# Startup of a fused attention and gMLP block: modulation weight rows, a turned conditioning vector, and separate banks for the first query copies

## Chip, cores, metric

One core of one Trainium2 chip. The metric is device time in microseconds of one execution. Times of one kernel spread by 0.7 us between its first three runs.

In the lines of the profile PE is TensorE, PEld its weight loads, DVE VectorE, ACT ScalarE, POOL GpSimd and SPq the queue of SyncE, which issues most transfers. L763 is line 763 of that run's kernel; the line numbers shift a little from kernel to kernel. A bank is a tile of 128 x 512 f32 in PSUM, where every matmul of this kernel writes its result. An x tile is 128 rows of x, and to turn a tile is to transpose it.

## The reference, cut to what matters

```python
mod = (_silu(c) @ w_mod).reshape(c.shape[0], 6, 1, -1)      # c: 1 x 512, w_mod: 512 x 3072
sa, ca, ga, sb, cb, gb = ...                                # six rows of 512
h = _layernorm(x) * (1 + ca) + sa                           # x: 1 x 2048 x 512
x = x + ga * _A_ref(h, K, V, wq, wo)                        # 32 query heads, 8 key heads, Dh 128
h = _layernorm(x) * (1 + cb) + sb
x = x + gb * _B_ref(h, w_in, w_sp, b_sp, w_out)             # gMLP
```

Nothing of the attention can start before the first two rows of `mod` (shift and scale) are known, the first 128 rows of x are normalised, modulated and turned, and their queries are projected. That preparation is what the change touches.

## The kernel before

The DMA loads of the start, in issue order. The modulation weight is read so that partition p holds rows 4p to 4p+3; c is read to match, eight bytes per partition:

```python
wmod_dram = w_mod.rearrange("(p dt) n -> p dt n", p=P)
c_dram = c[0].rearrange("(p j) -> p j", p=P)
...
nc.scalar.dma_start(out=c_bf[:], in_=c_dram)
nc.sync.dma_start(out=x_sb[:, 0, :], in_=x_dram[:, 0, :])
for kt in range(NDT):                                   # four parts of 256 KB
    nc.sync.dma_start(out=wmod_a[:, kt, :], in_=wmod_dram[:, kt, 0 : 2 * D])
load_k_nat(0)
...
load_wq(0, nc.sync)                                     # first query weights, 512 KB
load_k_nat(1)
nc.sync.dma_start(out=x_sb[:, 1:CT, :], in_=x_dram[:, 1:CT, :])
```

The in-order matmul program of the start. `warm(n)` issues n matmuls on zeros, whose result nobody reads; they are meant to keep TensorE's clock up. `bank("misc")`, `bank("o_ps")` and `bank2()` each rotate through two buffers, so what is written to a buffer waits until the readers of its last contents are done:

```python
warm(10)
for kt in range(NDT - 1):
    mod_part(kt, mc_ps)                                 # 8 matmuls of one column
    warm(2)
x_ps = []                                               # turn the normalised x tile 0
for half in range(2):
    x_ps.append(bank(("misc", "o_ps")[half])[:].bitcast(BF16))
    ...                                                 # two transposes each
mod_part(NDT - 1, mc_ps)
mod_copy(0, mc_ps)                                      # VectorE: shift and scale
...                                                     # hT: VectorE two blocks, ScalarE two
k_turn((0, 1, 2, 3), (nc.vector.tensor_copy, nc.scalar.copy))   # first keys
q_ps = bank2()                                          # ONE tile of two banks
for n, dt in enumerate((0, 2, 1, 3)):
    for hh in range(REP):
        c0 = hh // 2 * 512 + hh % 2 * P
        nc.tensor.matmul(q_ps[:, c0 : c0 + P], ...)     # 16 matmuls: first queries
for hf, copy in enumerate((nc.vector.tensor_copy, nc.scalar.copy)):
    copy(out=qTs[0][:, 2 * hf : 2 * hf + 2, 0:P], in_=q_ps[:, hf * 512 : ...])
warm(1)
```

After that the attention loop runs: scores, exponential, values, with the preparation of x tiles 1 to 3 filled in between.

## Time and profile before

| | before |
|---|---|
| time, median (lowest to highest) | 1325.91 us (1325.71 to 1326.42), 3 runs |
| span of the profiled run | 1324.6 us |
| TensorE busy | 99% |
| ScalarE, VectorE, GpSimd busy | 81%, 36%, 4% |
| TensorE's share of the chain that ended last | 98% |

The chain that ended last is followed back from the last instruction: at each step to whatever released it. Where TensorE carries 98% of it, the program is one stream of matmuls, and a change elsewhere can count only if it makes the stream start earlier or run with fewer gaps. The lines themselves stand in the prediction.

### The profile page before, as it was taken

The page shows a single profiled execution, that of the slowest core. Times are in us where ns is not written, and L with a number is a line of the kernel's source. Part 1 is how long each engine was busy: PE and PEld are TensorE (multiplying, and loading weights), DVE is VectorE, ACT ScalarE, POOL GpSimd, SP SyncE. Part 2 cuts the span into 40 slices and gives each one's busy share as a digit, 9 for nine tenths or more (in the row PEclk, how much of TensorE's full clock was granted, in tenths as well). Part 3 has the DMA queues.
Part 4 walks back from the last instruction along what each step waited for, and adds up shares of the span by engine and source line. Part 5 has one row for each costly group of instructions (what it writes and reads, how often), then busy time and mean ns, then how long its engine had stood idle before and what let it go on. Part 6 is the DMA issues. An engine that isn't in the chain of part 4 may idle for free.

```text
span 1324.6 us, 27877 instructions
## 1 busy us (share of the span) xinstructions
PE 1313.2 (99%) x12332; PEld 858.6 (65%) x12332; DVE 473.2 (36%) x1168; ACT 1077.8 (81%) x1061; POOL 49.4 (4%) x92
## 2 busy tenths in 40 slices
PE   8999999999999999999999999999999999999997
PEld 5666666666666666666666666666666666644444
DVE  5632222222222222222222222222222566793444
ACT  6898999999999999999999999999999999650000
POOL 1200000000000000000000000000000000120000
PEclk9999999999999999999999999999999999999999
DMA  7451022102111112111110221021101121143200
GB/s 179 123 122 33 13 49 37 37 13 53 28 26 33 34 37 37 30 36 37 33 37 14 53 37 33 17 52 24 31 13 21 25 34 33 29 116 83 64 21 27
DMA packets 148352, 58.12 MB, mean 44 GB/s; under 512 B 138400, under 2 KB 143904, under 8 KB 148224
## 3 DMA queue, kind: packets, MB, share of 16 engines
q1 hardware_dynamic: 141568, 37.84, 15.1%
q0 software_dynamic: 4208, 16.39, 4.4%
q10 hardware_dynamic: 2448, 2.03, 0.5%
q8 instruction: 98, 1.61, 0.5%
q14 instruction: 30, 0.25, 0.1%
HBM read 21.37 MB, written 2.10 MB: 18 GB/s over the span
## 4 chain that ended last, share of the span: by engine, by line
PE 98%; DMA 0%; DVE 0%; SPq 0%; issue 0%; ACT 0%
PE o_ps L1002 35%; PE s_ps L980 33%; PE misc L1034 8%; PE misc L947 8%; PE misc L1347 7%; PE s_ps L1193 2%; PE s_ps L1232 2%; PE o_ps L1368 1%; PE s_ps L1368 1%; DMA wq_g<-in_A_wq_dram 0%; PE misc L1104 0%; SPq L699 0%; PE misc L1355 0%; PE s_ps L921 0%; PE misc L846 0%; DVE yout L1384 0%
## 5 line engine op out<-in xcount | busy, mean ns | idle before, releaser
L987 ACT ACTIVATE pT<-s_ps 128x1024 bf16<-128x1024 f32 x1024 | 1044.5, 1025 | 83.4 <-PE s_ps L980 9.4
L1002 PEld LDWEIGHTS <-pT 128*128 128x128 bf16 x8192 | 548.5, 98 | 241.2
L1002 PE MATMUL o_ps<-v,pT 128*128 128x129 bf16 x8192 | 631.4, 220 | 0.0
L980 PE MATMUL s_ps<-qT,kT 128*128 128x512 bf16 x2048 | 609.9, 379 | 0.7 <-ACT qT L929 0.7
L1013 DVE RECIPROCAL rall<-o_ps 128x2 f32<-128x2 f32 x256 | 43.7, 171 | 744.4 <-PE o_ps L1002 744.2
L980 PEld LDWEIGHTS <-kT 128*128 128x128 bf16 x2048 | 199.5, 98 | 119.2 <-issue 1.4
L1034 PE MATMUL misc<-wo_g,oT 128*128 128x512 bf16 x512 | 194.0, 379 | 0.0
L947 PE MATMUL misc<-hT,wq_g 128*128 128x512 bf16 (+2 forms) x528 | 189.6, 371 | 0.0
L1014 DVE TENSOR_TENSOR onorm<-o_ps,rall 128x256 bf16<-128x256 f32 x256 | 108.7, 425 | 9.0 <-DVE rall L1013 0.3
L1347 PE MATMUL misc<-wsp,z 128*128 128x512 bf16 (+2 forms) x560 | 100.7, 336 | 0.0
L958 DVE CAST qT<-misc 128x512 bf16<-128x512 f32 x127 | 86.3, 680 | 2.0 <-PE misc L947 1.9
L1347 PEld LDWEIGHTS <-z 128*128 128x128 bf16 x560 | 50.6, 98 | 48.4
L1047 DVE TENSOR_TENSOR xacc<-misc,xacc 128x512 f32<-128x512 f32 x112 | 76.2, 680 | 0.0
L947 PEld LDWEIGHTS <-wq_g 128*128 128x128 bf16 x528 | 50.6, 98 | 1.1 <-issue 0.2
L1034 PEld LDWEIGHTS <-oT 128*128 128x128 bf16 x512 | 50.1, 98 | 0.8
L1362 DVE TENSOR_TENSOR gb<-misc,bsp_bc 128x512 bf16<-128x512 f32 (+1 forms) x28 | 18.4, 658 | 59.0 <-PE misc L1347 59.0
L1193 PE MATMUL s_ps<-win_sb,hT 128*128 128x448 bf16 x128 | 27.0, 352 | 0.0
L1203 ACT ACTIVATE z<-s_ps 128x896 bf16<-128x896 f32 x16 | 14.7, 917 | 14.9 <-PE s_ps L1193 14.9
L1232 PE MATMUL s_ps<-hT,win_sb 128*128 128x512 bf16 x112 | 24.5, 379 | 0.0
L1240 ACT ACTIVATE z1T<-s_ps 128x1024 bf16<-128x1024 f32 x14 | 14.3, 1024 | 10.0 <-PE s_ps L1232 9.1
L691 DVE BATCH_NORM_STATS2 bnst<-x_sb 128x6 f32<-128x512 bf16 x32 | 21.9, 683 | 0.5
L715 POOL DMA_DIRECT2D wq_g<-in_A_wq_dram x7 | 5.3, 753 | 420.9 <-PE misc L947 420.9
(86 smaller groups left out, 283.4 us busy)
## 6 DMA issues: line engine op xcount, KB each, us to landing
wq_g<-in_A_wq_dram POOLq DMA_DIRECT2D x7, 512.0 KB, 3.9
v<-in_A_v_cache_dram POOLq DMA_DIRECT2D x7, 512.0 KB, 7.1
wo_g<-in_A_wo_dram POOLq DMA_DIRECT2D x7, 512.0 KB, 4.8
oT<-onorm SPq DMA_TRANSPOSE x128, 2.4
wsp<-in_w_mod_dram POOLq DMA_DIRECT2D x1, 2048.0 KB, 10.4
out_dram<-yout ACTq DMA_DIRECT2D x15, 128.0 KB, 1.7
win_sb<-in_B_w_in_dram POOLq DMA_DIRECT2D x1, 1792.0 KB, 7.8
x_sb<-in_A_x_dram SPq DMA_DIRECT2D x3, 512.0 KB, 5.6
```

Source lines behind the costliest of these rows:

```text
L947: nc.tensor.matmul(ps[0][:, o0 : o0 + n], lhsT=wqs[g][:, dt, hh * DH : (hh + 1) * DH], rhs=hTs[ch][:, dt, c0 : c0 + n], start=(dt == 0), s ...
L958: nc.vector.tensor_copy(out=dst, in_=src)
L980: nc.tensor.matmul(s_ps[:, h * 512 : (h + 1) * 512].rearrange("p (r q) -> p r q", r=REP), lhsT=groups[g]["kT"][:, kt * P : (kt + 1) * P], ...
L987: nc.scalar.activation(out=pTs[u][:, 2 * i : 2 * i + 2, :], in_=s_ps[:].rearrange("p (k q) -> p k q", k=2), func=ACT.Exp, scale=inv_sqrt_dh,)
L1002: nc.tensor.matmul(o_ps[:, hh % 2, 0 : DH + 1], lhsT=pTs[u][:, kt, hh * P : (hh + 1) * P], rhs=groups[g]["v1"][:, kt, 0 : DH + 1], start=( ...
L1013: nc.vector.reciprocal(out=rall[:, c0 : c0 + 2], in_=o_ps[:, :, DH])
L1014: nc.vector.tensor_tensor(out=onorms[u][:, hh - 1 : hh + 1, :], in0=o_ps[:, :, 0:DH], in1=rall[:, c0 : c0 + 2].unsqueeze(2).to_broadcast([ ...
L1034: nc.tensor.matmul(X_ps[:], lhsT=oTs[u][:, hh, :], rhs=groups[g]["wo"][:, hh, :], start=(hh == 0), stop=(hh == REP - 1),)
L1047: nc.vector.tensor_tensor(out=xaccs[j][:], in0=X_ps[:], in1=xaccs[j][:], op=ALU.add)
L1193: nc.tensor.matmul(ps[0][:, hf * 512 : hf * 512 + FC], lhsT=h2Ts[j // CT][:, dt, (j % CT) * P : (j % CT + 1) * P], rhs=win_sb[:, dt, FH + ...
L1232: nc.tensor.matmul(ps[0][:, k * 512 : (k + 1) * 512], lhsT=win_sb[:, dt, f * P : (f + 1) * P], rhs=h2Ts[2 * ch2 + k][:, dt, :], start=(dt ...
L1347: nc.tensor.matmul(g_ps[:, :n], lhsT=z2[:, st, f * P : (f + 1) * P], rhs=wsp[t][:, st, c0 : c0 + n], start=(st == 0), stop=(st == NT - 1 a ...
```

## The change

Its intent: read each of the four modulation parts as 128 neighbouring rows, read c in one contiguous piece and turn it with a matmul against the identity, and let the two engines that copy the first queries work side by side. Half of the turned x moves from the bank of the key transposes to a score buffer, so that these transposes can run earlier. The change also adds warm-up matmuls around the first projection: four before it, one after.

```diff
-    wmod_dram = w_mod.rearrange("(p dt) n -> p dt n", p=P)
-    c_dram = c[0].rearrange("(p j) -> p j", p=P)
+    wmod_dram = w_mod.rearrange("(dt p) n -> p dt n", p=P)
+    c_dram = c[0].rearrange("(j p) -> j p", p=P)
...
+    warm(4)
+    c_ps = bank("misc")[:].bitcast(BF16)
+    nc.tensor.transpose(c_ps[:, 0:NDT], c_bf, ident[0:NDT, 0:NDT])
...                                     (the SiLU instructions move here, reading c_ps)
-    warm(10)
+    warm(6)
...
-        x_ps.append(bank(("misc", "o_ps")[half])[:].bitcast(BF16))
+        x_ps.append((bank("misc")[:] if half == 0 else bank2()[:, 0:512]).bitcast(BF16))
...
-    q_ps = bank2()
+    warm(4)
+    q_ps = [bank("misc"), bank("misc")]
...
-                q_ps[:, c0 : c0 + P],
+                q_ps[hh // 2][:, hh % 2 * P : (hh % 2 + 1) * P],
...
-            in_=q_ps[:, hf * 512 : hf * 512 + 2 * P].rearrange("p (h q) -> p h q", h=2),
+            in_=q_ps[hf][:, 0 : 2 * P].rearrange("p (h q) -> p h q", h=2),
-    warm(1)
+    warm(2)
```

More of the change, by code (lines that the diff above doesn't have):

```diff
@@ L692, in ln_stats @@
         nc.vector.bn_aggr(out=mv[:, j, :], in_=st[:])
-    c_bf = res.tile([P, NDT], BF16, name="c_bf")
-    nc.scalar.dma_start(out=c_bf[:], in_=c_dram)
+    c_bf = late.tile([P, REP, DH], BF16, name="onorm", bufs=3)[0:NDT, 0, :]
+    nc.scalar.dma_start(out=c_bf, in_=c_dram)
     nc.sync.dma_start(out=x_sb[:, 0, :], in_=x_dram[:, 0, :])
@@ L759 @@
     nc.vector.memset(ones_bf[:], 1.0)
-    c_f = res.tile([P, NDT], FP32, name="c_f")
-    nc.vector.tensor_copy(out=c_f[:], in_=c_bf[:])
-    en = res.tile([P, NDT], FP32, name="en")
-    nc.scalar.activation(out=en[:], in_=c_f[:], func=ACT.Exp, scale=-1.0)
-    nc.vector.tensor_scalar_add(out=en[:], in0=en[:], scalar1=1.0)
-    sig = res.tile([P, NDT], FP32, name="sig")
-    nc.vector.reciprocal(out=sig[:], in_=en[:])
-    sc = res.tile([P, NDT], FP32, name="sc")
-    nc.vector.tensor_tensor(out=sc[:], in0=c_f[:], in1=sig[:], op=ALU.mult)
-    sc_bf = res.tile([P, NDT], BF16, name="sc_bf")
-    nc.vector.tensor_copy(out=sc_bf[:], in_=sc[:])
     def warm(n):
@@ L886, in k_turn @@
             copy(out=kT0[:, part[0] * P : (part[-1] + 1) * P], in_=k_ps[:, 0 : n * P])
+    warm(4)
+    c_ps = bank("misc")[:].bitcast(BF16)
+    nc.tensor.transpose(c_ps[:, 0:NDT], c_bf, ident[0:NDT, 0:NDT])
+    c_f = res.tile([P, NDT], FP32, name="c_f")
+    nc.vector.tensor_copy(out=c_f[:], in_=c_ps[:, 0:NDT])
+    en = res.tile([P, NDT], FP32, name="en")
+    nc.scalar.activation(out=en[:], in_=c_f[:], func=ACT.Exp, scale=-1.0)
+    nc.vector.tensor_scalar_add(out=en[:], in0=en[:], scalar1=1.0)
+    sig = res.tile([P, NDT], FP32, name="sig")
+    nc.vector.reciprocal(out=sig[:], in_=en[:])
+    sc = res.tile([P, NDT], FP32, name="sc")
+    nc.vector.tensor_tensor(out=sc[:], in0=c_f[:], in1=sig[:], op=ALU.mult)
+    sc_bf = res.tile([P, NDT], BF16, name="sc_bf")
+    nc.vector.tensor_copy(out=sc_bf[:], in_=sc[:])
     xns0 = ln1_norm(0, 1, ln1_stats(0, 1))
     mc_ps = bank("misc")
-    warm(10)
+    warm(6)
     for kt in range(NDT - 1):
@@ L916 @@
     qTs = {0: early.tile([P, REP, 512], BF16, name="qT")}
-    q_ps = bank2()
+    warm(4)
+    q_ps = [bank("misc"), bank("misc")]
     for n, dt in enumerate((0, 2, 1, 3)):
         for hh in range(REP):
-            c0 = hh // 2 * 512 + hh % 2 * P
             nc.tensor.matmul(
-                q_ps[:, c0 : c0 + P],
+                q_ps[hh // 2][:, hh % 2 * P : (hh % 2 + 1) * P],
                 lhsT=wqs[0][:, dt, hh * DH : (hh + 1) * DH],
```

## The prediction

> **What bounds the kernel now.** I read the page first: the busy table, the 40 slices, then the shares of the chain that ended last.
>
> ```profile
> PE 1313.2 (99%) x12332; PEld 858.6 (65%) x12332; DVE 473.2 (36%) x1168; ACT 1077.8 (81%) x1061; POOL 49.4 (4%) x92
> PE   8999999999999999999999999999999999999997
> ...
> PE 98%; DMA 0%; DVE 0%; SPq 0%; issue 0%; ACT 0%
> ```
>
> TensorE is busy 99% of 1324.6 us and carries 98% of the chain. The list of waits from 30 us to the end shows no matmul of TensorE waiting (one weight load waits 0.4 us in the tail). So the kernel is one in-order matmul stream from about 15 us on, and only two stretches are not matmul: the first 15 us and a VectorE tail after 1316 us. The diff touches only the first. I compared the instruction order of both kernels on every engine: after the first exponentials the TensorE order is the same instruction for instruction, and the other engines keep their order throughout. So the most that the change can win is part of the first 15 us, about 1% of the time, and what it wins there moves the whole stream earlier one for one.
>
> Next the chain in order of time, over the first 15 us (start, length, what):
>
> ```profile
> 3.56 6.02 DMA wq_g<-in_A_wq_dram
> 9.59 0.05 issue
> 9.63 1.08 PE s_ps L921 x16
> 10.71 0.02 issue
> 10.74 0.44 DVE qT L929
> 11.17 0.02 issue
> 11.20 0.38 ACT qT L929
> 11.58 0.04 issue
> 11.62 1.01 PE s_ps L980 x2
> 12.63 0.44 PE o_ps L883 x4
> 13.07 0.02 issue
> 13.09 0.42 DVE kT L886
> 13.52 0.61 DVE bnst L691
> ```
>
> The first query weights land at 9.58; sixteen matmuls project the first 128 queries; VectorE copies two heads out of PSUM, and only then ScalarE copies the other two. Then two score matmuls take 1.01 us, where the same pair takes 0.43 on the chain after 15 us, four key transposes take 0.44, and a VectorE chain (key copy, statistics, normalisation) leads to the next transposes at 14.69.
>
> Why 1.01? The table of stretches has the granted clock (column before the last two):
>
> ```profile
> 11.00:11.20 0.20, 0.00 (x0) 0.00 (x0) 0.20 (x2) 0.01 (x1) 0.00 (x0) 1.00 1.28 291
> 11.20:11.40 0.20, 0.00 (x0) 0.00 (x0) 0.20 (x1) 0.20 (x1) 0.00 (x0) 0.68 1.31 280
> ...
> 14.50:15.00 0.50, 0.31 (x5) 0.31 (x6) 0.50 (x2) 0.47 (x1) 0.00 (x0) 0.81 1.08 344
> ```
>
> A mean of 0.68 over 0.2 us, between 1 and 0.5, puts the drop at 11.27; 0.81 over 0.5 us puts the return at 14.69. The stretches between show 0.50. So TensorE ran at half clock for 3.42 us.
>
> [...] the half-clock stretch is 3.42 us[...]; the warm-up matmuls do come every 0.43 us until about 4.5 and every 0.21 us after it (the clock column misses this first cold stretch). In the window from 7.86 to 11.27 TensorE worked only about 1.8 us: two transposes (0.27), the projection (1.07), one warm-up (0.38) and scraps.
>
> [...] In the kernel before the two query copies read different banks, yet ScalarE waited 1.56 us for VectorE's copy: the two banks were one two-bank tile, and ScalarE's copy carries a wait on VectorE. In the changed program it waits on TensorE alone. The trace thus shows a wait of the program, not of the hardware.
>
> [...] The old read of c is 128 packets of 8 bytes. The transfer view over the first 14 us gives its queue 0.5% of 16 engines: 14 x 16 x 0.005 = 1.1 us, or 0.07 us of each engine. So removing it is worth at most 0.07 us.
>
> **The change part by part.**
>
> 1. *c turned by TensorE.* Before, c landed 2.1 us after its issue at 0.73 and the SiLU chain ran on VectorE from 2.82 (first cast) to 4.04 (last cast). Now a transpose stands behind four warm-ups. Those start at 1.18, 0.43 us each, so it issues at about 2.9, and its 0.2 to 0.3 us of latency makes the chain start near 3.2: 0.4 us later, sc_bf at about 4.45. Its first reader started at 4.94, behind ten warm-ups, which stay ten. So nothing on the path. Statistics of the first x tile stand behind it on VectorE and move from 3.95 to about 4.4; the normalised tile from 6.28 to about 6.7; its transposes ran at 7.17. Hidden, but with only some 0.4 us left.
>
> 2. *Modulation parts of neighbouring rows.* Each part still moves 128 rows of 2 KB in one issue (0.43 us of queue). The stretches from 2.0 to 7.0 moved 279 GB/s on average, those from 7.5 to 9.5 moved 369 with the mixed traffic of later. If row order is the reason, parts 1 and 2, which held TensorE until 5.88 and 6.52 (1.0 us of waits), land some tenths earlier, and so does wq_g. I have no measurement of row order alone, so I count 0 here and put it in the range.
>
> 3. *Earlier key transposes, then four warm-ups.* The third and fourth key transposes waited for ScalarE until 8.96, since the turned x held their bank. It now lies in a score bank, so they run at about 7.8. Four warm-ups follow, in the bank that VectorE's key copy frees at 8.83: 4 x 0.215 = 0.86, so 8.87 to 9.73. The projection starts at 9.73 in place of 9.63: +0.10. But TensorE is now busy about 2.6 us of the 3.41, and I expect the clock to stay full at 11.27.
>
> 4. *Query copies in separate banks.* They run side by side: 0.38 + 0.02 off the chain, -0.40. With +0.10 from part 3 the first scores start at 11.32, not 11.62: -0.30.
>
> 5. *Full clock after that.* Two score matmuls: 0.43 on the chain in place of 1.01, -0.58. Four transposes: 4 x 0.056 + 0.16 = 0.38 against 0.44, -0.06. The VectorE key copy would start at 13.09 - 0.30 - 0.58 - 0.06 = 12.15. VectorE's statistics of x tile 1 (x landed at 4.59 + 6.4 = 10.99) end at about 12.10, just clear of it. The VectorE run after it, whose durations don't depend on TensorE's clock, brings the next transposes to 14.69 - 0.94 = 13.75. There the clock of before returns to full as well.
>
> Sum: -0.94 us. Nothing downstream takes it back: the transposed half of k lands at 5.27 + 6.7 = 12.0 and v by about 14.1, both before their first use (v at 21.4), and the exponentials move with their scores. 1325.91 - 0.94 = about 1325.0.
>
> **Rivals.**
>
> - *The clock still drops.* [...] Then part 5 falls away and only -0.30 is left: 1325.6. Against it: 2.6 busy microseconds of 3.41 rather than 1.8. One chance in four.
> - *The warm-ups get in the way.* If wq_g lands earlier, or VectorE's key copy frees the bank later, part 3 costs up to 0.5 us: 1325.5. For it: warm-ups are unconditional and in order. Against: wq_g at 9.59 is the gate today, within 0.14 us of their end.
> - *The row order is worth a lot.* If the parts came at 369 rather than 279 GB/s, a megabyte takes 2.8 rather than 3.8 us; the modulation, hT and the key copy move by perhaps 0.4 us, with the warm-ups behind them: 1324.5. For it: the slow rate while the strided parts run. Against: the transfer engines show 80 to 108% busy even then, so they were not starved, and x's normalisation bounds how far the modulation can move.
> - *The c path comes late.* Were the 256-byte rows slower to land than 2.1 us, TensorE would stall behind the transpose and everything shifts: 1326.4. [...]
>
> **Range and chances.** A fast-run spread of 0.7 us (1325.71 to 1326.42) and outcomes between 1324.5 and 1326 give 1324.0 to 1326.1. A gain of 2% would be 26 us, nearly twice everything before the dense stream, so same is all but certain; the remaining chances stand for a surprise of the chip.
>
> **What would show it.** Right: no half clock after 5 us; ScalarE's query copy beginning with VectorE's; the first scores at about 11.3, the transposes of x tile 1 at about 13.75, and every later matmul earlier by that shift. Wrong: 0.5 in the clock column near 12 us (part 5), the projection later than 9.8 behind warm-ups (part 3), modulation matmuls waiting for the SiLU chain (part 1), or the landing of the four parts moved by half a microsecond (part 2).

The expectation that the clock stays full at 11.27, on which the -0.64 of part 5 hangs, stands on TensorE's 2.6 us of work in 3.41 alone. The stretch from 7.86 to 11.27 is simply the 3.41 us before the clock fell, and that the work in it matters, here and in the first rival, was assumption, not shown. That VectorE's durations don't depend on TensorE's clock is in the traces: its key copy, statistics, their aggregation and the normalisation took 0.42, 0.61, 0.18 and 0.31 us on the chain at half clock (first trace of before) and the same at full clock (its second trace).

## The result, and the profile after

| | before | changed |
|---|---|---|
| median of six runs | 1325.83 us | 1325.97 us |
| lowest to highest | 1325.55 to 1326.42 | 1325.56 to 1326.26 |
| ratio of the fast runs | | 1.0, interval 0.9988 to 1.0013 |

A ratio is the mean time of one kernel's fast runs over that of the other's of the same rounds, so not quite the ratio of the medians. The verdict is the same time. The forecast range (1324.0 to 1326.1) holds it, but it held the unchanged kernel's time too; the forecast gain of 0.94 us is not there.

From the page of the changed kernel, the busy table and the chain's shares:

```profile
PE 1302.2 (98%) x12132; PEld 858.7 (65%) x12338; DVE 472.7 (36%) x1168; ACT 1077.6 (81%) x1061; POOL 48.9 (4%) x92
...
PE 98%; issue 1%; DVE 0%
```

Nothing has moved at this scale. (The lower busy time of TensorE isn't work saved: 12338 weight loads stand against 12132 matmuls, so some 200 matmul records are missing.) One thing is gone from the shares: before, DMA and SyncE's queue stood in the chain; now they don't. So the start of the chain has changed its nature. Here it is in order of time (start, length, what):

```profile
8.12 0.16 DVE modc L790
8.28 0.08 DVE modc L791
8.36 0.03 issue
8.39 0.60 DVE hT L815 x2
8.98 0.21 DVE kT L873
9.20 0.04 issue
9.24 0.38 PE o_ps L763
9.61 0.05 issue
9.67 0.59 PE o_ps L763 x2
10.26 0.89 PE misc L923 x16
11.15 0.43 PE o_ps L763 x2
11.59 0.03 issue
11.61 0.59 PE s_ps L982 x2
```

Before, the projection was released by the landing of the query weights. Now it stands behind warm-ups (L763), these behind VectorE's key copy (L873), this behind the modulated x (L815) and the modulation columns (L790). In the trace the first projection matmul starts at 10.10; before, at 9.63. The query weights had landed at 9.77.

The two query copies, from the timeline of the changed kernel (the bracket is the idle time before and what ended it):

```profile
11.08 0.42 DVE L931 CAST qT<-misc 128x256 bf16<-128x256 f32 x1 [1.90 <-PE misc L923]
11.19 0.37 ACT L931 CAST qT<-misc 128x256 bf16<-128x256 f32 x1 [1.67 <-PE misc L923]
```

They overlap, as intended. And the clock, from the table of stretches (column before the last two), in the place where the kernel before showed 0.50:

```profile
11.50:12.00 0.50, 0.47 (x3) 0.25 (x3) 0.50 (x2) 0.06 (x1) 0.00 (x0) 1.00 1.35 247
```

So both improvements that were forecast are to be seen in this trace, and so is a loss in front of them that was forecast at 0.10 and is about 0.5. In these two traces the transposes of x tile 1 start at 14.06 and 14.69: 0.63 earlier. Why, then, are six runs against six equal? The traced execution of before took 1326.34 us, near the top of its runs; the traced one of the changed kernel took 1325.56, the fastest of its six. Two single traces compared two extremes.

### The profile page after: what moved, and what is told of

The parts are those of the page before. It is cut to its first block, busy times and chain, and to the rows that moved or that the text cites. A ratio compares the mean times of both kernels' runs of the same rounds, so it can differ in the third digit from the quotient of the medians.

```text
span 1323.8 us, 27684 instructions
## 1 busy us (share of the span) xinstructions
PE 1302.2 (98%) x12132; PEld 858.7 (65%) x12338; DVE 472.7 (36%) x1168; ACT 1077.6 (81%) x1061; POOL 48.9 (4%) x92
## 4 chain that ended last, share of the span: by engine, by line
PE 98%; issue 1%; DVE 0%
PE s_ps L982 36%; PE o_ps L1004 35%; PE misc L1349 7%; PE misc L949 7%; PE misc L1036 6%; PE s_ps L1195 2%; PE s_ps L1234 2%; PE o_ps L1370 1%; PE o_ps L763 1%; PE s_ps L1370 0%; PE misc L1106 0%; PE misc L1357 0%; PE misc L833 0%; PE misc L923 0%; DVE yout L1386 0%
## 5 line engine op out<-in xcount | busy, mean ns | idle before, releaser
L949 PE MATMUL misc<-hT,wq_g 128*128 128x512 bf16 (+2 forms) x466 | 166.6, 370 | 0.1
L1036 PE MATMUL misc<-wo_g,oT 128*128 128x512 bf16 x386 | 146.3, 379 | 0.0
```

What stands on the lines that cost most here:

```text
L949: nc.tensor.matmul(ps[0][:, o0 : o0 + n], lhsT=wqs[g][:, dt, hh * DH : (hh + 1) * DH], rhs=hTs[ch][:, dt, c0 : c0 + n], start=(dt == 0), s ...
L1036: nc.tensor.matmul(X_ps[:], lhsT=oTs[u][:, hh, :], rhs=groups[g]["wo"][:, hh, :], start=(hh == 0), stop=(hh == REP - 1),)
```

## The experiments

Three theories went in. **W**: the added warm-ups wait for VectorE's key copy and hold up the projection, which eats what the copies win. **P**: the clock rises and falls at other times in every execution, so the half-clock stretch of the first trace isn't a property of the kernel before ("phase" in the expectations means these times). **R**: the new row order makes the transfers land earlier or later. Against them stood N (only chance) and D (something later takes the gain back).

The intervals that come with the ratios are about ±0.0014, or 1.8 us, in all runs, wider than anything told here; by them every run is "the same". I therefore lean on the traces, and use differences of mean times as support. The traces allow it because of one number. From the start of the transposes of x tile 1 to the end of the last matmul it took 1302.39 to 1302.41 us in 12 of the 14 traces, whatever the kernel (the two exceptions have VectorE's order changed and are told below). From there to the end of the span it took another 7.23 to 7.47 us. So the time is that start plus a constant, to within some 0.25 us, and theory D is out: nothing that is won before the transposes is lost in the matmuls after them.

All runs in one table. (The programs of one session ran on one chip, those of different sessions on different chips.) "Difference" is the mean of the kernel's five runs less the mean of the runs of before in the same session (nine; six for the first line); the other columns are of the one traced execution: when the clock rose from half to full (worked out from the warm-ups: in the first two traces they come every 0.43 us before it and every 0.22 us after), when the query weights landed, when the first projection matmul, the first scores and the transposes of x tile 1 started. From the scatter of the runs alone, the standard error of the differences is 0.13 to 0.30 us, so those up to 0.25 can't be told from nothing, while those of 0.56 and more are at least twice their error.

| run | median us | difference us | clock up | weights land | projection | scores | x tile 1 |
|---|---|---|---|---|---|---|---|
| before, first trace | 1325.91 | | 4.45 | 9.59 | 9.63 | 11.62 | 14.69 |
| changed, first trace | 1325.97 | +0.06 | 5.52 | 9.77 | 10.10 | 11.61 | 14.06 |
| before_again | 1325.68 | -0.09 | 4.73 | 9.63 | 9.68 | 11.66 | 14.11 |
| after_again | 1325.65 | -0.19 | 4.67 | 9.42 | 9.64 | 11.16 | 13.61 |
| banks_only | 1325.17 | -0.71 | 4.08 | 9.22 | 9.27 | 10.79 | 13.24 |
| no_added_warm | 1325.15 | -0.62 | 5.20 | 9.61 | 9.66 | 11.19 | 13.64 |
| warm_score_bank | 1325.21 | -0.61 | 5.78 | 10.28 | 10.32 | 11.85 | 14.30 |
| warm_doubled | 1326.59 | +0.64 | 6.17 | 9.61 | 11.16 | 12.68 | 15.13 |
| c_rows_only | 1325.52 | -0.25 | 5.50 | 9.45 | 9.49 | 11.48 | 13.93 |
| split_wq | 1324.23 | -1.41 | 5.52 | in halves | 9.06 | 10.86 | 13.53 |
| split_wq_again | 1324.71 | -1.21 | 4.58 | in halves | 8.96 | 10.52 | 13.12 |
| split_x_first | 1324.44 | -1.28 | 4.92 | in halves | 8.55 | 10.11 | 12.55 |
| split_and_swap | 1325.51 | -0.56 | 5.94 | in halves | 9.12 | 10.69 | 13.23 |
| split_swap_x_first | 1325.14 | -0.90 | 5.93 | in halves | 8.96 | 10.52 | 12.71 |

### before_again: the unchanged kernel

No edit.

> The unchanged kernel once more, for a second trace. Theory P [...]: the clock rises at another time than 4.45 us, the half-clock stretch of 3.41 us near 12 us moves or is missing, and the start of the transposes of x tile 1 (14.69 us in the first trace) moves with it, by up to 1 us; the times spread over 0.7 us or more with no change of the program. Theory D (downstream or program effect, phase of no weight): rise again near 4.45, drop again near 11.3, transposes at 14.69 within 0.15.

The chain of this second trace, where the first showed 1.01 and 0.44:

```profile
11.66 0.59 PE s_ps L980 x2
12.25 0.24 PE o_ps L883 x4
```

The first scores start where they did (11.66, 11.62), but the clock stays full, and the transposes of x tile 1 come 0.58 us earlier, with no change of the program. That is what the forecast had booked under full clock (0.64), and here the kernel before has it by itself. The work before it was much the same: in the stretch from 3.41 to 6.82 us after the rise of the clock, at whose end it fell in the first trace, TensorE worked 1.63 us there (7.86 to 11.27) and 1.73 us here (8.14 to 11.56, after which the clock stayed). How often does it lack it? A granted clock of 0.997 or less over a whole run means, by my estimate, at least 6.6 us at half clock (under 0.9975 after rounding, so a loss of 0.0025 x 1324 us or more, each half-clock us losing half; the first trace has 3.42 + 5.98 us at half and 0.996); the stretch at the end, after the matmuls, accounts for 3.3 to 6.0 us in the traces. So such a run had another stretch. Of the 36 runs of before beside the experiments 5 have it (1326.13 to 1327.88 us), of the 5 runs here none. About one execution in eight. Theory P holds.

### after_again: the changed kernel

No edit.

> The changed kernel once more. Theory P: the rise is elsewhere than 5.52 us, and the first modulation matmuls move with it (5.59 in the first trace; about 5.0 if the rise comes before 4.6); ratio to before 1.000 with a difference within 0.4 us, either sign. Theory R (the new row order makes parts 2 and 3 and the query weights land later): the parts land again at about 3.9, 5.2, 6.8 and 7.5 us and the query weights at 9.8, whatever the clock does.

The clock rose at 4.67 in place of 5.52. The first modulation matmuls moved from 5.59 to 5.17, the projection from 10.10 to 9.64, the transposes by 0.45. So the changed kernel's start depends on the clock: its chain leads back through warm-ups and modulation to the first warm-up. The fixed landings that theory R expected are not there (the third part landed at 6.09, not 6.83). The difference to before, -0.19, is within the 0.4 of theory P.

### banks_only: the copies alone

```diff
-    q_ps = bank2()
+    q_ps = [bank("misc"), bank("misc")]
```

with the addresses of the matmuls and copies to match; all else as before.

> The kernel before with the two query copies in separate banks and nothing else. All theories: ScalarE's copy starts within 0.15 us of VectorE's, so the first scores start 0.4 us earlier after the end of the projection (0.51 after its last matmul in place of 0.91). Theory P: the clock near 12 us is a matter of the execution; time 0.0 to 0.4 us below before. If the forecast of parts 3 and 5 was right (the warm-ups are what keeps the clock), the gain here is 0.3 to 0.4 and the changed kernel lies another 0.5 below.

The chain, from the issue of the query weights:

```profile
3.56 5.66 DMA wq_g<-in_A_wq_dram
9.22 0.04 issue
9.27 1.08 PE misc L920 x16
10.35 0.02 issue
10.37 0.38 ACT qT L928
10.75 0.04 issue
10.79 0.59 PE s_ps L979 x2
```

The landing still releases the projection, and one copy, not two, lies between it and the scores. From the start of the last projection matmul to the first scores it takes 0.68 us (10.11 to 10.79); before, 1.14 (10.48 to 11.62, and the same in the second trace). So the separate banks win 0.46 us. The mean time fell by 0.71, more than that and more than the expected 0.0 to 0.4; this trace also had an early landing (9.22), so part of the rest may be chance.

### no_added_warm: the change without its added warm-ups

```diff
-    warm(4)
     q_ps = [bank("misc"), bank("misc")]
...
-    warm(2)
+    warm(1)
```

> The changed kernel without the four warm-ups ahead of the projection and with one rather than two after it. Theory W (those four cost: they wait for VectorE's key copy, and the projection waits for them): the projection starts as soon as the query weights or the turned x are there, 0.3 to 0.5 us earlier than in the changed kernel in the same phase; time 0.2 to 0.5 us below the changed kernel, unless the clock drops near 12 us, which costs about 0.6. Theory of the forecast: the drop comes in most executions and the time is 0.2 to 0.6 us above the changed kernel.

The projection starts at 9.66, 0.05 after the landing of the weights at 9.61, although the key copy ends at 9.29, later than in either trace of the changed kernel with its 9.18 and 8.72. With the warm-ups it would have started 0.92 after that copy, at 10.21. The mean (1325.16) is 0.42 below that of after_again (1325.59) in the same session, with a standard error of 0.16. The edit also takes out the second warm-up behind the projection, but that one costs nothing: from the last projection matmul to the first scores it takes 0.67 us with it (10.94 to 11.61) and 0.68 without (10.51 to 11.19). None of the five runs shows a clock of 0.997 or less. So the four warm-ups cost time, and here at least they were not needed to keep the clock: theory W as it stands in the expectation, while the opposite that the forecast implied, 0.2 to 0.6 us more than the changed kernel, did not come.

### warm_score_bank: the same warm-ups, waiting for nothing

```diff
-    def warm(n):
+    def warm(n, w_ps=None):
-        w_ps = bank("o_ps")
+        w_ps = bank("o_ps") if w_ps is None else w_ps
...
-    warm(4)
+    warm(4, bank2()[:, 0:512])
```

> The changed kernel with its four warm-ups written to the second score buffer, which is free, so that they wait for no copy. Theory W (the wait for VectorE's key copy puts them on the path): they run right behind the key transposes, end before 9.4 us, and the projection starts at the landing of the query weights (9.2 to 9.7 us); time 0.4 to 0.6 us below before, as without them. Theory N (what the changed kernel loses is chance of the execution): no clear difference from the changed kernel, which was within 0.1 us of before.

The median is as without them (1325.21), the mean 0.61 below before. The traced execution, the slowest of its five, happened to have very late landings: the third modulation part at 7.91, the query weights at 10.28. It shows the wait gone all the same: the first recorded one starts at 9.49, well before the key copy ends at 10.26, and the projection at 10.32, 0.06 after that end in place of 0.92. (The last warm-up ends together with the landing, so this trace doesn't tell which of the two released the projection.) With the mean, it says that not the warm-ups' work costs, but their place behind the key copy. The expected landing range (9.2 to 9.7) was missed.

### warm_doubled: eight in place of four

```diff
-    warm(4)
+    warm(8)
     q_ps = [bank("misc"), bank("misc")]
```

> The changed kernel with eight warm-ups ahead of the projection in place of four. Theory W: each of them is on the path and costs its 0.215 us, so 0.86 us more than the changed kernel: 0.7 to 0.9 us above before, and the projection starts 1.7 to 1.8 us after the end of VectorE's key copy in place of 0.9. Theory N, or any in which the query weights' landing still sets the start: under 0.4 us more.

```profile
11.32 0.89 PE misc L923 x16
12.22 0.43 PE o_ps L763 x2
12.65 0.03 issue
12.68 0.59 PE s_ps L982 x2
```

The weights had landed at 9.61; the projection starts at 11.16, which is 1.78 after the end of the key copy (9.38). In the two traces of the changed kernel that distance is 0.92. Four more warm-ups, 0.86 us more, one for one. The mean is 0.64 above before, where the expectation said 0.7 to 0.9; against after_again's -0.19 (another session) the four cost 0.83.

### c_rows_only: rows and turned c alone

The changed kernel with `x_ps`, `q_ps` and the warm-ups around the projection as before.

> The changed rows of the modulation weight and the turned c alone, with the buffers and warm-ups of before. Theory W with no gain from row order: the query weights land at 9.2 to 9.8 us as in all runs so far and gate the projection, the copies stay serial; time within 0.25 us of before. Theory R (rows cost or win): the landing moves outside that range, or the time by more than 0.3 us.

The weights landed at 9.45 and the projection started at 9.49, though in the chain of this trace it stands behind ScalarE's work on the turned x and the last key transposes, which arrived together with the landing; the copies are serial again (0.46 apart). The mean lies 0.25 below before, at the edge of the expectation, and with five runs I can't tell it from nothing. Over all traces with the query weights in one piece, they landed at 9.59, 9.63 and 9.22 with the old rows (mean 9.48), and at 9.77, 9.42, 9.61, 10.28, 9.61 and 9.45 with the new ones (mean 9.69). The modulation parts themselves show no gain either: the last of the four landed at 7.14, 7.70 and 6.89 with the old rows, and at 6.54 to 8.59 (mean 7.43) with the new ones in these traces. No gain of bandwidth is to be seen. The first trace's hint that strided rows are slow (279 GB/s from 2.0 to 7.0 us, 369 from 7.5 to 9.5) is not borne out.

### split_wq and split_wq_again: the gate itself

If the landing of the query weights is the gate, half of the projection can run before the last half lands:

```diff
-        engine.dma_start(out=wqs[g][:], in_=wq_dram[:, :, ...])
+        for d0, d1 in ((0, 2), (2, 4)) if g == 0 else ((0, 4),):
+            engine.dma_start(out=wqs[g][:, d0:d1, :], in_=wq_dram[:, d0:d1, ...])
...
-    for n, dt in enumerate((0, 2, 1, 3)):
+    for n, dt in enumerate((0, 1, 2, 3)):
```

on top of no_added_warm.

> The changed kernel without the added warm-ups, with the first query weights read in two halves (two of the four blocks of rows each), and the sixteen matmuls in the order of arrival. If the landing of the query weights is what sets the first scores, eight matmuls (0.45 us) run before the second half lands: first scores 0.3 to 0.45 us earlier than without the split, 0.8 to 1.0 us below before. If the landing of x tiles 1 to 3 (11.0 us) sets the pace by then, or the extra 0.43 us of issue delays the loads behind it, the gain is under 0.2.

> The halves alone once more, to see whether 1324.23 us was chance: its five times went from 1323.95 to 1325.19. If real: median 1324.0 to 1324.9, at least 0.8 us below before of the same session. If chance: 1325.1 or more, like the kernel without the added warm-ups.

The means are 1.41 and 1.21 below before, and no run of the ten is slower than 1325.19. The lowest of the 18 runs of before in these two sessions is 1325.26, so the two sets do not overlap: a version that is ahead of both kernels, by 0.1%. Against no_added_warm's -0.62, on which it is built, the halves are worth 0.6 to 0.8 us; the two never ran in one session, so that size is rough. In the first trace the gate has moved on:

```profile
5.04 6.07 DMA x_sb<-in_A_x_dram
11.12 0.02 issue
11.14 0.70 DVE bnst L691
```

x tiles 1 to 3 land at 11.12, VectorE's statistics start there, and the scores at 10.86 no longer matter.

### split_and_swap, split_swap_x_first, split_x_first: the next gate

The first puts VectorE's normalisation of x tile 1 ahead of the statistics of tile 2, the second also issues x tiles 1 to 3 ahead of the second half of the keys, the third has that issue order without the swap:

```diff
+    nc.sync.dma_start(out=x_sb[:, 1:CT, :], in_=x_dram[:, 1:CT, :])
     load_k_nat(1)
-    nc.sync.dma_start(out=x_sb[:, 1:CT, :], in_=x_dram[:, 1:CT, :])
```

> The kernel with the query weights read in halves, and VectorE's normalisation of x tile 1 ahead of the statistics of x tile 2. In the trace of the halves alone the chain ran from the landing of x tiles 1 to 3 (11.12 us) through 0.70 + 0.20 + 0.31 + 0.61 + 0.20 + 0.31 us of VectorE to the transposes of x tile 1 at 13.53. The swap takes the second statistics (0.81) out but GpSimd's root takes about 1 us from the end of the first: transposes 2.1 us after the landing in place of 2.4, time 0.2 to 0.4 us below the halves alone, 1.3 to 1.8 below before. If the root is not back by then, under 0.1.

> As the one before, and x tiles 1 to 3 are issued ahead of the second half of the keys. The landing of x moves up by about 0.35 us (128 KB at 370 GB/s), to some 10.7; first scores (10.4 to 10.9) become the gate together with it; time 0.1 to 0.35 us below the run before this one. If the keys then land after 11.4 us, the key transposes wait and nothing is won.

> The halves, and x tiles 1 to 3 issued ahead of the second half of the keys, with the order on VectorE left alone. The run with the swap had x land at 9.89 us in place of 10.81, but the modulation of the turned x, last on VectorE, came no earlier. Here the chain from x is the old one, 2.4 us from the later of the landing and VectorE's query copy to the transposes: 10.4 + 2.5 = 12.9 to 13.1 in place of 13.5. Time 0.3 to 0.5 us below the halves alone; no gain if the keys become the gate (transposes of keys later than 11.7).

The swap missed, on both sides of the transposes. They came no sooner: 2.42 us after the landing of x (10.81 to 13.23), as with the halves alone (2.41 and 2.42), because the wait for GpSimd's root took the place of the statistics; with x first they started at 12.71, later than the 12.55 without the swap. And the way from there to the last matmul grew from 1302.40 to 1303.20 us in both. In its chain the turned x is now modulated behind two statistics on VectorE, and the next projection, of x tile 1, waits for that. Medians 1325.51 and 1325.14: nothing was won ahead of the transposes, and 0.80 us was lost behind them. Without the swap, x first landed x at 9.98 in place of 11.12 and 10.70, and its transposes started at 12.55, the earliest of all; its median is 1324.44 and its mean (-1.28) is no better than the halves alone (-1.41, -1.21). But the traced execution (1324.18) was the fastest of its five, while those of the halves (1325.19 and 1324.76) were the slowest of theirs: once more single traces compared extremes. Whether x first gains anything stays open.

## Why the prediction was right or wrong

**The range**: it held because it was wide. It ran from 1324.0 to 1326.1 and so took in no change at all; that it was met says nothing for the sum.

**The bound**: right. The stream after the start is a constant 1302.40 us, and what is won in front of it arrives at the end.

**Part 1, turned c**: right in its times. SiLU was done at 4.43 in place of 4.04 (forecast 4.45), the normalised tile at 6.68 (forecast 6.7), and neither released anything. It overlooked that the transpose stands in TensorE's own stream: the fifth warm-up starts at 3.11 in place of 2.86, and the chain of the changed kernel leads through it. At nearly the same rise of the clock (4.73 and 4.67) the first modulation matmul starts at 5.08 in before_again and at 5.17 in after_again, so about 0.1 us.

**Part 2, rows**: counted as 0, and that is what the landings show (mean 9.48 with the old rows, 9.69 with the new).

**Part 3, the four warm-ups**: this step failed first. Forecast "+0.10"; the runs of one session give 0.42 between the changed kernel and the one without the added warm-ups. The term was mis-sized because the forecast took the key copy's end, 8.83, from one trace. It ended at 9.18 and 8.72 in the changed kernel and as late as 9.39 in before_again, and in both traces of the changed kernel the projection started 0.92 after it. In the kernel before, a late key copy did not hold the projection: in the first trace only the weights' landing held the projection, and in the second a late modulation chain arrived together with it (9.63 and 9.68). What the part said of the key transposes was right: they ran at 7.95, not 8.96. The change moved the path off a transfer and onto a chain of matmuls whose pace depends on when the clock rises: at 4.67 in place of 5.52, the projection at 9.64 in place of 10.10. The forecast named this rival (1325.5) and its mechanism, but gave it too little.

**Part 4, separate banks**: right in kind and size: 0.40 forecast, 0.46 measured. (The 1.56 us that ScalarE is said to have waited for VectorE's copy is its whole idle time before; the copy held it for 0.46, from 10.74 to 11.20.)

**Part 5, full clock**: this step failed for good. The saving of "-0.58" and "-0.06" was read off one execution as if it were the kernel's. That a half-clock stretch costs this much is right: the two traces of before differ by 0.58 at the transposes. But its two terms were both off and the errors cancelled, which is luck: at full clock the first two score matmuls took 0.59 us on the chain, not 0.43 (so -0.42), and the four transposes 0.24, not 0.38 (so -0.20). And only about one run of before in eight has the half-clock stretch, so removing it always would be worth 0.64 / 8, about 0.1 us on average. (The five such runs lie 1.05 us above the mean of the other 36, which makes 0.13.) The rival "the clock still drops" asked how sure the clock was in the changed kernel. The question that was not asked is how sure the drop was in the kernel before. That TensorE's work decides on the clock was assumed, and no run here shows it. The work was misread as well: TensorE was busy for 1.63 us of the stretch from 7.86 to 11.27, not 1.8 (the sum counts the overlap of the warm-up with the projection twice), and with 1.73 in before_again the clock stayed. Whether the added warm-ups make drops rarer isn't settled: none of 11 runs of the changed kernel has one, but neither has any of the 10 of banks_only and no_added_warm. In their traces the stretch from 3.41 to 6.82 us after the rise, which holds the projection, had 3.03 and 2.77 us of work with the warm-ups (forecast 2.6), and 1.95 and 2.12 without them; the first two score matmuls took 0.59 us, as at full clock, in all four.

**The sum** as the runs have it: the change without the added warm-ups -0.62, the warm-ups +0.42, together -0.19 (rounded means) in that session and +0.06 in the first. The forecast said -0.94.

## What to carry to other kernels

A single trace is one draw: between two traces of the same kernel the transposes of x tile 1 moved by 0.58 us here. Before booking a clock drop or a landing time as a saving, look whether the unchanged kernel has it in a second trace, and in the granted clock of all its runs. Filler matmuls ahead of the work cost something here (0.42 us for four) when what they waited for came late; the same four in a buffer that no one had to empty left a mean 0.61 below before, about that of the kernel without them (-0.62 in another session). And when the gate is a transfer, cut the transfer, so that work can begin with its first half: here the means fell to 1.41 and 1.21 below before, against 0.62 without the cut.

## Clock and landings in these traces

- The warm-ups began at 1.18 us, and in the 14 traces of the table the clock rose at 4.08 to 6.17, so 2.9 to 5.0 us after them.
- In the first trace the clock halved for 3.42 us after a stretch in which TensorE worked 1.63 of 3.41 us. The work in such a stretch doesn't tell here whether the clock falls: with 1.73 us it stayed (before_again), and at the end of the first trace it fell after 1.85 (1315.17 to 1318.58). The price in this kernel was 0.58 us at the transposes.
- A landing varies from execution to execution: the same 512 KB, issued at 3.55 to 3.56 us behind transfers of the same sizes, landed between 9.22 and 10.28 us.
